# Six padded attention chunks, zero matmuls, split weight casts, and a last output tile in three column parts

## The chip, the cores and the metric

The kernel runs on one core of one Trainium2 chip. The metric is device time in microseconds (us), lower is better. Each kernel was run several times, always beside runs of the kernel before on the same chip. Runs have a state, fast or slow. The time is about 1.8 us longer than the "span" of the profile, which goes from the first instruction to the last.

Ratios are computed as the mean time of one kernel's fast runs over the mean of the other's of the same rounds, so they are not quite the ratio of the medians that are quoted. Intervals are 95%. A kernel counts as faster or slower when it differs by over 2%.

Engine names: PE is the TensorE matmul, PEld its weight load, DVE is VectorE, ACT is ScalarE, POOL is GpSimd, SP is SyncE, which here issues almost all DMAs.

## The reference

Attention with a decaying state, over 4 sequences of 768 tokens with 8 heads of 64 numbers, followed by a dense network of two layers:

```python
for b in range(nb):                       # blocks of 64 tokens
    intra = einsum('bhic,bhjc->bhij', qb, kb) * Dmask          # Dmask: lam ** (i - j), causal
    intra = einsum('bhij,bhjd->bhid', intra, vb)
    inter = einsum('bhid,bhde->bhie', qb * lam_pow, kv_state)
    out[:, :, sl] = intra + inter
    kv_state = lam_block * kv_state + einsum('bhsd,bhse->bhde', kb_dec, vb)
x = out.transpose(0, 2, 1, 3).reshape(3072, 512)
h = x @ w_in                              # 512 -> 2048
g = h * sigmoid(h)                        # silu
y = g @ w_out                             # 2048 -> 512, result 3072 x 512 float32
```

## The kernel before

The kernel works in bf16 on chunks of 128 tokens (24 of them) with float32 sums. Attention of a later group of chunks runs between the matmuls of the dense layers of an earlier group, so that PE always has something to do. The first group has four chunks; its attention is the start of the kernel.

Two heads share the 128 rows of PE. The first `N0 = 4` chunks use a *padded* layout: the values of a pair of heads lie in `vpad` beside zeros, and one ACT or DVE cast puts them there. All later chunks use *halves*: a cast to `vb`, then four DVE copies (`spread_v`) into a buffer that was cleared before. Halves need less PE time; padding needs no spreading. Buffers are used in turn, `c % 4`.

```python
NKV = 4                                   # vpad, ktbd, kvbd: four buffers each, cleared at the start
def spread_v(c):                          # only chunks that are not padded
    if c in vnew:
        vnew.discard(c)
        vb, vh = natb[c][2], vhalf[c % NKV]
        for j in range(2):
            for h in range(2):
                nc.vector.tensor_copy(vh[64*j:64*j+64, :, h, j, :], vb[64*h:64*h+64, :, j, :])

def pe_s(c, j, tag="att"):                # scores; a padded chunk takes all 128 columns
    qt, kt = tr[c]
    a = 0 if c < N0 else 64 * j
    # [...] four matmuls, one per pair of heads

def ffn1(g, m, ...):                      # one 128-row tile of h, then silu on ACT
def ffn2(g, mt, kos, tag="o"):            # out tile of 128 tokens x 512, 16 matmuls, DVE copy, store
    # [...]
    if kos[-1] == KO_OUT - 1:
        ob = opool.tile([128, DM], F32, tag="ob")
        nc.vector.tensor_copy(ob, o)
        stores.append([0, out[r0:r0 + BLK, :], ob])      # issued by SP a little later
def op_z(n, tag="kv"):                    # matmuls of zeros that nobody reads: they keep PE busy
    zero = kvbd[NKV - 1]
    for i in range(n):
        nc.tensor.matmul(wt, lhsT=zero[:, 0, :], rhs=..., start=True, stop=True)   # 512 columns

# the start is a list of words, executed in order: z zero matmuls, tq/tk transposes, s scores, m masks,
# d state, o output, x its cast, w:i cast of piece i of w_in, f:part,half first layer
ORDER = "z:8 pq:0,1,P pq:0,0,D tq:0,h [...] w:0,D d:2 [...] f:0,0 x:3,A w:1,D kv:3,A f:0,1 f:1,0 f:1,1 w:2,D w:3,D"

# the first switch from padding to halves, in program order
clear_halves()                            # POOL clears all four buffers again
[...]
st_s(5)
vcast(4), vcast(5)
spread_v(4), spread_v(5)                  # 8 copies on DVE
down0(3, 2)                               # dense layer 2, last quarter
st_d(4)
down0(3, 3)
st_o(4); st_d(5); next_prep()
down0(3, 0)
st_o(5); next_prep()
down0(3, 1)
stretch((ups(1), 0, 1), ([(vcast, 6), (spread_v, 6)], 0.0, 0.1), (pieces(2), 0.2, 1.15), ...)
[...]
for unit in downs(len(GROUPS) - 1, range(nch[-1])):      # the last tiles
    unit[0](*unit[1:])
tick(0)                                   # store of the last tile
```

## Time and profile before

| | before |
|---|---|
| time | 221.94 us median of 3 (221.92 to 222.25) |
| span of the profiled run | 219.35 us |
| PE busy | 205.9 us, 94% |
| first matmul; full clock in the trace's record from | 3.15; 11.87 us |
| first layer starts; its second group of matmuls | 20.64; 22.07 us |
| first matmul of group 1; scores of chunk 6 | 54.97; 59.56 us |
| end of PE; end of span | 215.61; 219.35 us |

The page of the kernel before, parts 1, 2 and 4 (busy time of an engine with its share and count; PE's busy tenths in 40 slices; the chain of waits by engine):

```profile
PE 205.9 (94%) x1595; PEld 127.4 (58%) x1595; DVE 122.5 (56%) x264; ACT 102.7 (47%) x213; POOL 62.1 (28%) x68
PE   4878999996799999999999999999999999999993
...
PE 83%; DVE 10%; ACT 3%; DMA 2%; issue 1%; POOL 1%; DVEq 0%
```

PE bounds the kernel. There are gaps only in three places, which the windows of the kernel before show (stretch in us, its length, then busy time of PE, PEld, DVE, ACT, POOL with instruction counts, clock, DMA share, GB/s):

```profile
0.00:22.00 22.00, 15.94 (x143) 10.22 (x143) 18.45 (x33) 13.75 (x26) 16.81 (x25) 1.00 1.04 234
...
43.00:66.00 23.00, 19.70 (x198) 14.12 (x196) 19.21 (x43) 12.53 (x27) 9.11 (x9) 1.00 1.20 232
66.00:100.00 34.00, 33.83 (x318) 24.52 (x316) 27.55 (x60) 17.59 (x43) 12.18 (x12) 1.00 1.18 202
100.00:208.00 108.00, 108.00 (x793) 64.44 (x791) 46.60 (x114) 49.29 (x101) 17.33 (x17) 1.00 0.59 117
208.00:219.00 11.00, 7.61 (x38) 3.43 (x35) 2.08 (x3) 0.38 (x1) 0.00 (x0) 1.00 0.18 72
```

PE lacks 6 us of work in the first 22 us, 3.3 us between 43 and 66, and the tail after 215.6 us has none. From 66 to 208 us it lacks 0.2 us in all.

The start, from the timeline of PE and DVE before (start, us, engine, line, operation, out<-in, count; in brackets the idle time before it and what ended it):

```profile
3.15 3.60 PE L489 MATMUL warm_ps<-kvbd 128*128 128x512 bf16 x8 [3.15 <-DVE kvbd L108]
...
21.10 0.92 DVE L159 CAST w_in_bf<-w_tmp 128x1024 bf16<-128x1024 f32 x1
...
22.07 1.16 PE L417 MATMUL h_ps<-xt,w_in_bf 128*128 128x256 bf16 x9 [0.39 <-DVE w_in_bf L159]
```

The second w_in piece landed at 20.20 us, but DVE reached its cast at 21.10. The middle, in the same views:

```profile
48.68 3.31 DVE L274 COPY vpad<-vb 64x256 bf16<-64x256 bf16 x8
...
50.84 0.55 PE L394 MATMUL op<-ss,vpad 128*128 128x128 bf16 x8 [0.61 <-DVE vpad L274]
...
53.54 0.40 PE L394 MATMUL op<-qt,kvbd 128*128 128x128 bf16 x4 [1.29 <-DVE kvbd L159]
...
54.97 2.11 PE L417 MATMUL h_ps<-xt,w_in_bf 128*128 128x256 bf16 x16
...
55.90 2.39 DVE L274 COPY vpad<-vb 64x256 bf16<-64x256 bf16 x4
...
59.56 0.51 PE L363 MATMUL sp<-qt,ktbd 128*128 128x128 bf16 x8 [1.16 <-DVE ktbd L159]
```

Spreading occupies DVE while PE waits, once for the copies themselves and twice for casts queued behind them. The tail, timeline before:

```profile
212.91 3.79 SPq L435 DMA_DIRECT2D out_dram<-ob  x2
215.64 0.69 DVE L447 COPY ob<-o_ps 128x512 f32<-128x512 f32 x1 [2.76 <-PE o_ps L443]
```

After the last matmul come a copy of 0.69 us and the second of these two stores, issued at 216.36 and landed 2.01 us later.

### The profile page before, as it was taken

What the parts mean: (1) busy time and instruction counts of PE and PEld (TensorE: products, weight loads), DVE (VectorE), ACT (ScalarE), POOL (GpSimd) and SP (SyncE); (2) the same over time, 40 slices, a digit from 0 to 9 for tenths busy, and PEclk for the clock granted to TensorE, in tenths of its full rate; (3) what the DMA queues carried; (4) which work ended last, traced back from release to release, by engine and by line L of the source; (5) the groups of instructions that cost most, each with busy time, mean ns of one, the idle gap of its engine ahead of it and who ended that gap; (6) DMA issues with size and microseconds to landing.
All of it is one profiled execution on the core that took longest, in us unless ns stands there. A gap on an engine that the chain in (4) does not pass through costs nothing.

```text
span 219.3 us, 4154 instructions
## 1 busy us (share of the span) xinstructions
PE 205.9 (94%) x1595; PEld 127.4 (58%) x1595; DVE 122.5 (56%) x264; ACT 102.7 (47%) x213; POOL 62.1 (28%) x68
## 2 busy tenths in 40 slices
PE   4878999996799999999999999999999999999993
PEld 1456644553695777775665566556655565566641
DVE  7699555089888768886686564436571341100021
ACT  4685564142673555655554454445445434433300
POOL 7579600716333332323333334203000000000000
PEclk9999999999999999999999999999999999999999
DMA  4999999999999999999999999949510011011112
GB/s 122 242 221 351 381 387 341 263 232 219 234 232 187 215 194 175 220 202 197 190 173 215 240 169 233 201 115 190 107 48 34 14 51 49 0 51 48 48 56 88
DMA packets 97652, 38.03 MB, mean 173 GB/s; under 512 B 86880, under 2 KB 90976, under 8 KB 97632
## 3 DMA queue, kind: packets, MB, share of 16 engines
q1 hardware_dynamic: 97488, 37.76, 81.1%
q8 instruction: 12, 0.20, 0.4%
q14 instruction: 8, 0.07, 0.1%
q10 hardware_dynamic: 144, 0.00, 0.0%
HBM read 27.27 MB, written 6.29 MB: 153 GB/s over the span
## 4 chain that ended last, share of the span: by engine, by line
PE 83%; DVE 10%; ACT 3%; DMA 2%; issue 1%; POOL 1%; DVEq 0%
PE o_ps L443 37%; PE h_ps L417 35%; PE op L394 5%; PE sp L363 4%; DVE ss L370 3%; DVE vpad L274 2%; DMA lam_sb<-in_lam_dram 2%; PE kv_ps L339 2%; ACT g L421 1%; DVE ktbd L159 1%; DVE ob L447 1%; DVE w_in_bf L159 1%; POOL qb L232 1%; DVE vpad L159 1%; ACT L127 1%
## 5 line engine op out<-in xcount | busy, mean ns | idle before, releaser
L421 ACT ACTIVATE g<-h_ps 128x256 bf16<-128x256 f32 (+2 forms) x144 | 65.1, 456 | 79.5 <-PE h_ps L417 78.1
L417 PE MATMUL h_ps<-xt,w_in_bf 128*128 128x256 bf16 (+2 forms) x592 | 99.9, 304 | 1.0 <-DVE w_in_bf L159 0.7
L443 PE MATMUL o_ps<-w_out_bf,g 128*128 128x512 bf16 x384 | 95.8, 379 | 0.2 <-DVE w_out_bf L159 0.2
L417 PEld LDWEIGHTS <-w_in_bf 128*128 128x128 bf16 x592 | 55.4, 98 | 32.6 <-issue 1.3
L443 PEld LDWEIGHTS <-g 128*128 128x128 bf16 x384 | 36.4, 98 | 32.2 <-issue 0.3
L447 DVE COPY ob<-o_ps 128x512 f32<-128x512 f32 x24 | 16.5, 691 | 47.1 <-PE o_ps L443 47.0
L243 POOL TENSOR_TENSOR qb<-qf,lam_fwd 128x512 bf16<-128x512 f32 x18 | 19.0, 1055 | 67.9 <-DMA qf<-in_q_dram 63.3
L370 DVE TENSOR_TENSOR ss<-sp,mask 128x512 bf16<-128x512 f32 (+1 forms) x48 | 25.7, 575 | 17.2 <-PE sp L363 16.5
L274 DVE COPY vpad<-vb 64x256 bf16<-64x256 bf16 x80 | 29.0, 362 | 1.8
L237 POOL TENSOR_TENSOR kb<-kf,lam_bwd 128x512 bf16<-128x512 f32 x23 | 24.3, 1060 | 6.0 <-DMA kf<-in_k_dram 4.1
L159 DVE CAST kvbd<-kv_ps 64x256 bf16<-64x256 f32 x32 | 13.5, 421 | 9.6 <-PE kv_ps L339 9.4
L402 ACT ACTIVATE xt<-op 128x512 bf16<-128x512 f32 x20 | 11.9, 597 | 11.0 <-PE op L394 10.3
L363 PEld LDWEIGHTS <-ktbd 128*128 128x128 bf16 x192 | 11.8, 100 | 6.2 <-DVE ktbd L159 2.9
L363 PE MATMUL sp<-qt,ktbd 128*128 128x128 bf16 (+1 forms) x192 | 13.7, 213 | 1.7 <-DVE ktbd L159 1.6
L394 PE MATMUL op<-ss,vpad 128*128 128x128 bf16 (+1 forms) x192 | 12.5, 208 | 0.6 <-DVE vpad L274 0.6
L157 ACT ACTIVATE vb<-vf 128x512 bf16<-128x512 f32 x20 | 12.5, 624 | 0.7 <-DMA vf<-in_v_dram 0.6
L159 DVE COPY ktbd<-kn 64x512 bf16<-64x512 bf16 x32 | 12.2, 382 | 0.8 <-DMA kn<-kb 0.5
L394 PEld LDWEIGHTS <-vpad 128*128 128x128 bf16 x192 | 10.7, 98 | 1.1 <-DVE vpad L274 0.8
L232 POOL TENSOR_TENSOR qb<-qf,lam_fwd 128x512 bf16<-128x512 f32 x4 | 4.6, 1166 | 16.6 <-DMA qf<-in_q_dram 15.0
L394 PE MATMUL op<-qt,kvbd 128*128 128x128 bf16 x80 | 7.7, 219 | 1.3 <-DVE kvbd L159 1.3
L159 DVE CAST w_in_bf<-w_tmp 128x1024 bf16<-128x1024 f32 x8 | 6.2, 781 | 3.8 <-DMA w_tmp<-in_moe_w_in_dram 3.8
L489 PE MATMUL warm_ps<-kvbd 128*128 128x512 bf16 x11 | 5.3, 632 | 3.2 <-DVE kvbd L108 3.2
(58 smaller groups left out, 85.4 us busy)
## 6 DMA issues: line engine op xcount, KB each, us to landing
kf<-in_k_dram SPq DMA_DIRECT2D x24, 256.0 KB, 4.8
vf<-in_v_dram SPq DMA_DIRECT2D x24, 256.0 KB, 5.1
out_dram<-ob SPq DMA_DIRECT2D x24, 256.0 KB, 3.1
qf<-in_q_dram SPq DMA_DIRECT2D x18, 256.0 KB, 3.7
w_tmp<-in_moe_w_in_dram SPq DMA_DIRECT2D x8, 512.0 KB, 8.6
w_tmp<-in_moe_w_out_dram SPq DMA_DIRECT2D x8, 512.0 KB, 10.1
qf<-in_q_dram SPq DMA_DIRECT2D x3, 512.0 KB, 5.9
qt<-qb SPq DMA_TRANSPOSE x16, 3.7
```

Source lines behind the costliest of these rows:

```text
L157: nc.scalar.activation(dst, src, AF.Copy)
L159: nc.vector.tensor_copy(dst, src)
L237: VG[e].tensor_tensor(kb, rawk.pop(c).rearrange("s (p j) d -> s p j d", j=2), decay(lam_bwd, c % NB), op=AL.mult)
L243: nc.gpsimd.tensor_tensor(qb, rawq.pop(c).rearrange("s (p j) d -> s p j d", j=2), decay(lam_fwd, c % NB), op=AL.mult)
L274: nc.vector.tensor_copy(vh[64 * j:64 * j + 64, :, h, j, :], vb[64 * h:64 * h + 64, :, j, :])
L363: nc.tensor.matmul(sp[:, p, :], lhsT=lhsT, rhs=qt[:, p, a:], start=True, stop=True)
L370: VG[e].tensor_tensor(ss, sp, m[:, None, :n].to_broadcast([128, 4, n]), op=AL.mult)
L394: nc.tensor.matmul(dst, lhsT=lhsT, rhs=rhs, start=(i == 0), stop=(i >= len(terms) - NP), skip_group_check=True)
L417: nc.tensor.matmul(hp[:, a:z], lhsT=w_in_bf[:, ko, m * 128:(m + 1) * 128], rhs=xt[g][:, ko, a:z], start=(ko == 0 and a == 0), stop=(ko == ...
L421: nc.scalar.activation(gg, hp[:, :n], AF.Silu)
L443: nc.tensor.matmul(o, lhsT=gt[g, ko][:, mt * BLK:(mt + 1) * BLK], rhs=w_out_bf[:, ko, :], start=(ko == 0), stop=(ko == KO_OUT - 1))
L447: nc.vector.tensor_copy(ob, o)
```

## The change

The intent has four parts.

1. *Padding to six chunks.* `NPAD = 6` in place of `N0 = 4`, so chunks 4 and 5 need no spreading. Their buffers 0 and 1 are then cleared for halves only after chunk 5 is done. The spread of chunk 6 moves later.
2. *Zero matmuls.* The zeroed weights come first, 15 zero matmuls instead of 8 at the start, and more in waits: 26 in all instead of 11, so that PE's clock rises early and stays up.
3. *Split casts.* The first two w_in pieces are cast half by DVE and half by ACT.
4. *Last tile in parts.* Columns 0–256, 256–384 and 384–512 each have their own bank, copy and store, so the last copy and store are small.

The core of the diff, with cuts marked:

```diff
+NPAD = 6
-z:8 pq:0,1,P pq:0,0,D tq:0,h [...] w:0,D d:2 kv:2,A o:2,att x:2,D
-d:3 o:3,att f:0,0 x:3,A w:1,D kv:3,A f:0,1 f:1,0 f:1,1 w:2,D w:3,D
+z:15 pq:0,1,P pq:0,0,D tq:0,h pk:0,D pk:1,P z:2 tk:0,o z:2 [...] z:1 [...] z:2 [...] z:1,o [...] z:2,o [...]
+o:2,att x:2,D w:0,DA z:1,o d:3 o:3,att f:0,0 x:3,A w:1,DA kv:3,A f:0,1 f:1,0 f:1,1 w:2,D w:3,D
+    nc.vector.memset(kvbd[NKV - 1], 0.0)          # the zero weights, now first
     def cast_w(which, i, e="D"):
-        move(e, w_piece(...), wtmp.pop((which, i)))
+        dst, t = w_piece(...), wtmp.pop((which, i))
+        n = dst.shape[1] // len(e)
+        for h, x in enumerate(e):
+            move(x, dst[:, n * h:n * h + n, :], t[:, n * h:n * h + n, :])
     [... c < N0 becomes c < NPAD at eight places; st_s uses mask if c < NPAD else mask2 ...]
-    clear_halves()
+    clear_halves(2, 3)
     [...]
     vcast(4), vcast(5)
-    spread_v(4), spread_v(5)
     [...]
     st_o(5)
     next_prep()
+    clear_halves(0, 1)
     down0(3, 1)
-    stretch((ups(1), 0, 1), ([(vcast, 6), (spread_v, 6)], 0.0, 0.1), (pieces(2), 0.2, 1.15),
+    stretch((ups(1), 0, 1), ([(vcast, 6)], 0.0, 0.1), ([(spread_v, 6)], 0.42, 0.42), (pieces(2), 0.2, 1.15),
+    def ffn2_last(g, mt):
+        for i, (a, z, tag) in enumerate([(0, 256, "o"), (256, 384, "h"), (384, 512, "h")]):
+            o = psum.tile([128, 512], F32, name="o_part", tag=tag, bufs=2)
+            [... 16 matmuls into o[:, :z - a] ...]
+            move("A" if i == 1 else "D", ob[:, :z - a], o[:, :z - a])
+            tick(0)
+            nc.sync.dma_start(out=out[r0:r0 + BLK, a:z], in_=ob[:, :z - a])
-    for unit in downs(len(GROUPS) - 1, range(nch[-1])):
+    for unit in downs(len(GROUPS) - 1, range(nch[-1] - 1)):
         unit[0](*unit[1:])
-    tick(0)
+    ffn2_last(len(GROUPS) - 1, nch[-1] - 1)
```

More of the change, by code (lines that the diff above doesn't have):

```diff
@@ L21 @@
 NQ2 = 6
+NPAD = 6
 ORDER = """
-z:8 pq:0,1,P pq:0,0,D tq:0,h pk:0,D pk:1,P tk:0,o z:1 kt:0,1,D qt:0,A kt:0,0,D qt:1,A s:0,1,o tk:1,h m:0,1,D pq:2,0,D
-s:0,0,att z:2 pq:2,1,P kt:1,0,A s:1,0,o tq:2,att kt:1,1,A pk:2,P m:0,0,D qt:2,A s:1,1,h vc:0,A tk:2,att m:1,0,D
-m:1,1,D d:0 qt:3,A pk:3,P kt:2,1,D s:2,1,h kt:2,0,D kv:0,A o:0,att s:2,0,h m:2,1,D tk:3,o m:2,0,D vc:1,A d:1 x:0,A
-kt:3,0,D kv:1,A s:3,0,att o:1,att kt:3,1,D s:3,1,h vc:2,D m:3,0,D vc:3,D x:1,A m:3,1,D w:0,D d:2 kv:2,A o:2,att x:2,D
-d:3 o:3,att f:0,0 x:3,A w:1,D kv:3,A f:0,1 f:1,0 f:1,1 w:2,D w:3,D
+z:15 pq:0,1,P pq:0,0,D tq:0,h pk:0,D pk:1,P z:2 tk:0,o z:2 kt:0,1,D qt:0,A kt:0,0,D qt:1,A s:0,1,o z:1 tk:1,h m:0,1,D
+pq:2,0,D s:0,0,att z:2 pq:2,1,P kt:1,0,A s:1,0,o tq:2,att kt:1,1,A pk:2,P m:0,0,D qt:2,A s:1,1,h vc:0,A tk:2,att
+m:1,0,D m:1,1,D d:0 qt:3,A pk:3,P kt:2,1,D s:2,1,h kt:2,0,D kv:0,A o:0,att s:2,0,h m:2,1,D z:1,o tk:3,o m:2,0,D vc:1,A
+z:2,o d:1 x:0,A kt:3,0,D kv:1,A s:3,0,att o:1,att kt:3,1,D s:3,1,h vc:2,D m:3,0,D vc:3,D x:1,A m:3,1,D d:2 kv:2,A
+o:2,att x:2,D w:0,DA z:1,o d:3 o:3,att f:0,0 x:3,A w:1,DA kv:3,A f:0,1 f:1,0 f:1,1 w:2,D w:3,D
 """
@@ L106 @@
         nc.vector.memset(vpad[i], 0.0)
-        if i == 1:
-            nc.vector.memset(kvbd[NKV - 1], 0.0)
         nc.vector.memset(ktbd[i], 0.0)
@@ L161, in cast_w @@
     def cast_w(which, i, e="D"):
-        move(e, w_piece(which, i, None, w_in_bf if which == "in" else w_out_bf), wtmp.pop((which, i)))
+        dst, t = w_piece(which, i, None, w_in_bf if which == "in" else w_out_bf), wtmp.pop((which, i))
+        n = dst.shape[1] // len(e)
+        for h, x in enumerate(e):
+            move(x, dst[:, n * h:n * h + n, :], t[:, n * h:n * h + n, :])
     mask2 = const.tile([128, BLK], F32)
@@ L170, with clear_halves @@
     khalf = [t.rearrange("d p j s -> d p (j s)").rearrange("d p (h j s) -> d p h j s", h=2, j=2) for t in ktbd]
-    def clear_halves():
-        for i in range(NKV):
+    def clear_halves(*bufs):
+        for i in bufs:
             nc.gpsimd.memset(ktbd[i], 0.0)
             nc.gpsimd.memset(vpad[i], 0.0)
-        for j in range(2):
-            nc.gpsimd.tensor_copy(mask2[64 * j:64 * j + 64, :], mask[0:64, :])
     NBUF = {"att": 3, "h": 2, "o": 2, "kv": 1}
@@ L190 @@
     xt = {}
-    N0 = GROUPS[0] // BLK
     def load_q(c):
@@ L238, in prep_k @@
                                 op=AL.mult)
-        natb[c] = (None, kb, vpad[c % NKV] if c < N0 else nat.tile([128, NP, 2, D], BF16, name="vb", tag="vb", bufs=2))
+        natb[c] = (None, kb, vpad[c % NKV] if c < NPAD else nat.tile([128, NP, 2, D], BF16, name="vb", tag="vb", bufs=2))
     def prep(c):
@@ L248, in vcast @@
     def vcast(c, e="A"):
-        if c in vraw and c >= N0:
+        if c in vraw and c >= NPAD:
             vb = natb[c][2]
@@ L284, in move_k @@
         rows = slice(64 * j, 64 * j + 64)
-        if c < N0:
+        if c < NPAD:
             move(e, ktbd[c % NKV][rows, :, j, :], t[rows, :, :])
@@ L304, in copy_qt @@
              tp[:, :, :, 64 * i:64 * i + 64].rearrange("d r p s -> d p s r"))
-        tr[c] = (qt, ktbd[c % NKV] if c < N0 else khalf[c % NKV])
+        tr[c] = (qt, ktbd[c % NKV] if c < NPAD else khalf[c % NKV])
     def pe_tk(c, tag):
@@ L338, in pe_d @@
         for p in range(NP):
-            nc.tensor.matmul(kv[:, p, :], lhsT=kb[:, p, :, :], rhs=vb[:, p, 0:4:3, :] if c < N0 else vb[:, p, :, :],
+            nc.tensor.matmul(kv[:, p, :], lhsT=kb[:, p, :, :], rhs=vb[:, p, 0:4:3, :] if c < NPAD else vb[:, p, :, :],
                              start=(blk == 0 and p == 0), stop=True, skip_group_check=True)
@@ L358, in pe_s @@
         qt, kt = tr[c]
-        a = 0 if c < N0 else 64 * j
+        a = 0 if c < NPAD else 64 * j
         sp = psum.tile([128, NP, BLK - a], F32, name="sp", tag=tag, bufs=NBUF[tag], padded_shape=[128, NP, BLK])
         for p in range(NP):
-            lhsT = kt[:, p, j, :] if c < N0 else kt[:, p, j, :, :]
+            lhsT = kt[:, p, j, :] if c < NPAD else kt[:, p, j, :, :]
             nc.tensor.matmul(sp[:, p, :], lhsT=lhsT, rhs=qt[:, p, a:], start=True, stop=True)
@@ L374, in st_s @@
         spread_k(c)
-        st[c] = [masked(pe_s(c, j), m=mask2) for j in range(2)]
+        st[c] = [masked(pe_s(c, j), m=mask if c < NPAD else mask2) for j in range(2)]
     def pe_o(c, tag="att"):
@@ L387, in pe_o @@
         for j in range(2):
-            if c < N0:
+            if c < NPAD:
                 terms += [(vb[:, p, 2 * j:2 * j + 2, :], res[j][:, p, :], op[:, p, :]) for p in range(NP)]
@@ L449, in ffn2 @@
             stores.append([0, out[r0:r0 + BLK, :], ob])
+    def ffn2_last(g, mt):
+        r0 = gstart[g] + mt * BLK
+        for i, (a, z, tag) in enumerate([(0, 256, "o"), (256, 384, "h"), (384, 512, "h")]):
+            o = psum.tile([128, 512], F32, name="o_part", tag=tag, bufs=2)
+            for ko in range(KO_OUT):
+                nc.tensor.matmul(o[:, :z - a], lhsT=gt[g, ko][:, mt * BLK:(mt + 1) * BLK], rhs=w_out_bf[:, ko, a:z],
+                                 start=(ko == 0), stop=(ko == KO_OUT - 1))
+            ob = opool.tile([128, DM], F32, name="ob", tag="ob")
+            move("A" if i == 1 else "D", ob[:, :z - a], o[:, :z - a])
+            tick(0)
+            nc.sync.dma_start(out=out[r0:r0 + BLK, a:z], in_=ob[:, :z - a])
     nch = [n // BLK for n in GROUPS]
@@ L514, in next_prep @@
                 load_c(loads.pop(0))
-    clear_halves()
+    clear_halves(2, 3)
+    for j in range(2):
+        nc.gpsimd.tensor_copy(mask2[64 * j:64 * j + 64, :], mask[0:64, :])
     for i in range(4, 8):
```

## The prediction

> **What bounds the kernel now.** TensorE is busy 94% of the 219.3 us span (page, engine table); the chain of waits puts 83% on PE. By stages (windows): from 66 to 208 us PE is busy 141.8 of 142 us, so nothing is to be had there. The change can win at three places: 0–22 us (PE busy 15.9 of 22, DVE 18.5), 43–66 us (PE 19.7 of 23), and the tail after 208 us.
>
> **Start.** Matmuls begin at 3.15 us at half pace (128 columns every 107 ns); the trace's first clock record, and a pace of 56 ns, begin at 11.87 us. The Trainium skill, "TensorE: Matmul & The Clock Gate", Part 1, says the gate opens after one busy free-running window of about 3.4 us; the trace agrees: PE is broken by idle pieces from 6.5 to 8.4 us, then nearly unbroken for 3.4 us. The zeroed weights now come first on DVE (ready near 1.3 us instead of 3.1) and 15 padding matmuls follow, so I expect full clock between 5 and 8.3 us. That shortens tk and sp on the chain by about 0.35 us; DVE paces the rest (busy 90–100% from 11 to 22). Later padding only fills waits. Split casts: the second w_in half is ready near 21.3 instead of 22.02 us (its DMA lands at 20.2), so ffn1's second group starts 0.65 us earlier. Later weight pieces land every 1.36 us, still in time.
>
> **43–66 us.** The spread copies of chunks 4 and 5 (8 DVE copies, 3.31 us at 48.7) vanish. They caused PE waits of 0.61 us (vpad) and 1.29 us (kvbd queued behind them); the spread of chunk 6 (2.39 us at 55.9), now behind the masks, caused 1.16 us (ktbd, 59.56). Against this: two masks grow from 415 to 689 ns, and the w_out cast queued behind them lets the last quarter of down-projection start only 0.3 us earlier. Walking both queues with these durations, ffn1 of group 1 starts at 52.7 instead of 54.97 us and sp of chunk 6 at 56.5 instead of 59.56. Kept by 66 us: 2.8 us. Clearing buffers 0 and 1 on POOL (four memsets of 0.95–1.5 us) now precedes chunk 8's preparation, which slips from 58 to about 61 us; its transposes were issued at 61.3 anyway: a few tenths at most.
>
> **Tail.** Before: last matmul ends 215.6, copy 0.69 us, store issued 216.36, landed 218.37. After: about 0.1 us more on PE; last copy 128 columns (estimate 0.29 us, from the 691 ns of 512 columns and 259 ns of 96); last store 64 KB instead of 256. "DMA: Bandwidth & Descriptors" puts most of a small transfer into a fixed part; the trace has 2.0 us for 256 KB, so I count 0.3 us off. Tail gain 0.6 us.
>
> **Sum.** 2.8 + 0.6 = 3.4 us: 218.5 us, 217.2 to 219.9. Chances: faster 0.15, within 2% 0.84, slower 0.01.
>
> **What would show it.** Clock record before 8.5 us; ffn1's second group near 21.4; no vpad copies at 48–52; PE idle in 43–66 falling from 3.3 to about 1 us; 66–208 unchanged but 2.8 us earlier; last copy 0.3 us, last landing 1.7 us after issue.
>
> **What would make it wrong.** DMA arrivals (loads of chunks 6–9 land 3.6–5 us apart, DMA share over 0.9 until 145 us) stalling the pulled-in PE at 60–80 us; POOL memsets slowing DVE spread copies (0.94 to 2.4 us under POOL work); the clock window falling late, so that padding delays tk; or DVE's queue giving more at the start than I count.

## The result, and the profile after

The kernel after takes 219.59 us (median of 4 runs, 219.19 to 220.11) against 222.09 us (4 runs, 221.92 to 222.26) of the kernel before: ratio 0.9891, interval 0.9864 to 0.9918. A second measurement, a0_again below, gave 0.9932, 0.9907 to 0.9957. By these two measurements the change saves 1.5 to 2.5 us, under 2%.

The profiled run, at 220.11 us the slowest of the four (spans of the other three: 217.5 to 217.8 us), is set against a profiled run of the kernel before that took 221.05 us, less than any of its timed runs. So these two profiles, whose spans are 1.03 us apart, understate the change. The profiled run after has this page (parts 1, 2 and 4 again):

```profile
PE 207.6 (95%) x1642; PEld 129.7 (59%) x1642; DVE 109.8 (50%) x257; ACT 103.9 (48%) x216; POOL 59.7 (27%) x68
PE   7778899999899999999989999999999999999994
...
PE 47%; DMA 30%; SPq 14%; POOL 5%; issue 1%; DVE 1%; POOLq 0%
```

Slice 10 is now full and slice 11 nearly so, and slice 21, full before, now has an 8. The chain of waits no longer lies on PE alone: 44% of it are DMAs and their issue. The windows after, of the stretches that changed:

```profile
0.00:22.00 22.00, 17.07 (x158) 10.36 (x158) 16.99 (x33) 13.85 (x26) 14.00 (x23) 1.00 1.03 233
...
43.00:66.00 23.00, 21.70 (x221) 15.76 (x219) 16.72 (x37) 12.51 (x27) 13.21 (x14) 1.00 1.17 233
...
100.00:208.00 108.00, 107.08 (x781) 63.60 (x779) 43.85 (x113) 48.33 (x99) 18.71 (x18) 1.00 0.63 123
```

Busy PE time does not tell progress here, as zero matmuls count as busy. A ledger does: the same instruction in several profiles, as its shift against the kernel before (a minus is earlier). The expected column is worked out from the prediction; "again" is a0_again, "best" is g1_dveclear, an experiment below.

| instruction | before, us | expected | after | again | best |
|---|---|---|---|---|---|
| second group of the first layer | 22.07 | −0.65 | +0.41 | +0.13 | +0.10 |
| first layer of group 1 begins | 54.97 | −2.27 | −1.42 | −1.66 | −1.66 |
| scores of chunk 6 | 59.56 | −3.06 | −1.82 | −2.06 | −2.06 |
| second layer of group 1 begins | 65.85 | −2.8 | −1.32 | −0.93 | −2.06 |
| last scores | 179.91 | −2.8 | −0.14 | −0.72 | −1.66 |
| end of PE | 215.61 | −2.7 | −0.06 | −0.64 | −1.58 |
| end of span | 219.35 | −3.4 | −1.03 | −1.62 | −2.57 |

The gain of the middle is there, but smaller, the start gained nothing, and in the profiled run most of the middle's gain went away before the last scores.

*Start.* The trace's record of full clock begins at 4.55 us instead of 11.87. The timeline of PE and DVE after:

```profile
1.26 5.02 PE L504 MATMUL warm_ps<-kvbd 128*128 128x512 bf16 x15 [1.26 <-DVE kvbd L104]
...
21.88 0.54 DVE L160 CAST w_in_bf<-w_tmp 128x512 bf16<-128x512 f32 x1 [1.76 <-DMA w_tmp<-in_moe_w_in_dram]
...
22.48 0.72 PE L419 MATMUL h_ps<-xt,w_in_bf 128*128 128x256 bf16 x5 [1.25 <-DVE w_in_bf L160]
```

DVE is now free at 20.1 us and waits 1.76 us for the second w_in piece, which landed at 21.85 us; before, it landed at 20.20.

*Middle.* No spreading at 48 us; the timeline of PE, DVE and POOL after:

```profile
53.55 1.67 PE L419 MATMUL h_ps<-xt,w_in_bf 128*128 128x256 bf16 x12
...
57.74 0.51 PE L365 MATMUL sp<-qt,ktbd 128*128 128x128 bf16 x8 [0.41 <-DVE ktbd L160]
...
58.32 1.04 POOL L245 TENSOR_TENSOR qb<-qf,lam_fwd 128x512 bf16<-128x512 f32 x1
...
59.17 1.76 DVE L276 COPY vpad<-vb 64x256 bf16<-64x256 bf16 x4
...
63.08 0.51 PE L365 MATMUL sp<-qt,ktbd 128*128 128x128 bf16 x8 [0.32 <-DVE ktbd L160]
```

The wait at 59.56 us before fell from 1.16 to 0.41 us, and a new one of 0.32 us came at 63.08 us. The preparation of chunk 8, at 55.6 us before, now stands at 58.32 behind the four memsets.

*Late.* A wait that the kernel before has not, in the timelines of DVE and PE:

```profile
112.15 0.59 DVE L160 COPY ktbd<-kn 64x512 bf16<-64x512 bf16 x2 [2.90 <-DMA kn<-kb]
...
112.80 0.51 PE L365 MATMUL sp<-qt,ktbd 128*128 128x128 bf16 x8 [0.92 <-DVE ktbd L160]
```

The same scores before, timeline of PE:

```profile
112.95 0.50 PE L363 MATMUL sp<-qt,ktbd 128*128 128x128 bf16 x8
```

The transposed keys of chunk 15 landed at 112.13 us, 5.11 us after their issue; before, at 108.62, 2.81 us after it. What the record shows of the difference is told at g3_best below.

*Tail.* The timeline after:

```profile
214.25 1.99 SPq L464 DMA_DIRECT2D out_dram<-ob  x3
214.69 0.28 ACT L158 ACTIVATE ob<-o_part 128x128 f32<-128x128 f32 x1 [5.65 <-PE o_part L459]
215.59 0.29 DVE L160 COPY ob<-o_part 128x128 f32<-128x128 f32 x1 [1.36 <-PE o_part L459]
```

From the end of PE to the end of the span it takes 2.77 us instead of 3.74. The last store of 64 KB landed 1.56 us after its issue.

### The profile page after: what moved, and what is told of

The parts are those of the page before. It is cut to its first block, busy times and chain, and to the rows that moved or that the text cites. A ratio compares the mean times of both kernels' runs of the same rounds, so it can differ in the third digit from the quotient of the medians.

```text
span 218.3 us, 4252 instructions
## 1 busy us (share of the span) xinstructions
PE 207.6 (95%) x1642; PEld 129.7 (59%) x1642; DVE 109.8 (50%) x257; ACT 103.9 (48%) x216; POOL 59.7 (27%) x68
## 4 chain that ended last, share of the span: by engine, by line
PE 47%; DMA 30%; SPq 14%; POOL 5%; issue 1%; DVE 1%; POOLq 0%
PE o_ps L445 22%; PE h_ps L419 19%; DMA qf<-in_q_dram 16%; SPq L209 8%; DMA w_tmp<-in_moe_w_in_dram 5%; DMA w_tmp<-in_moe_w_out_dram 5%; POOL qb L245 4%; SPq L263 3%; DMA kn<-kb 2%; PE op L396 2%; SPq L153 2%; DMA kf<-in_k_dram 2%; PE o_part L459 2%; PE sp L365 1%; POOL kb L239 1%
## 5 line engine op out<-in xcount | busy, mean ns | idle before, releaser
L445 PE MATMUL o_ps<-w_out_bf,g 128*128 128x512 bf16 x368 | 92.3, 379 | 0.3 <-DVE w_out_bf L160 0.3
L445 PEld LDWEIGHTS <-g 128*128 128x128 bf16 x368 | 34.9, 98 | 30.5 <-issue 0.5
L449 DVE COPY ob<-o_ps 128x512 f32<-128x512 f32 x23 | 15.9, 692 | 43.5 <-PE o_ps L445 43.4
L276 DVE COPY vpad<-vb 64x256 bf16<-64x256 bf16 x72 | 18.3, 254 | 1.6
L160 DVE COPY ktbd<-kn 64x512 bf16<-64x512 bf16 x32 | 10.8, 339 | 10.7 <-DMA kn<-kb 10.4
L365 PEld LDWEIGHTS <-ktbd 128*128 128x128 bf16 x192 | 11.2, 98 | 6.9 <-DVE ktbd L160 3.9
L158 ACT ACTIVATE vb<-vf 128x512 bf16<-128x512 f32 x18 | 11.2, 622 | 0.0
L234 POOL TENSOR_TENSOR qb<-qf,lam_fwd 128x512 bf16<-128x512 f32 x4 | 4.6, 1166 | 20.1 <-DMA qf<-in_q_dram 18.5
L504 PE MATMUL warm_ps<-kvbd 128*128 128x512 bf16 x26 | 8.5, 453 | 1.3 <-DVE kvbd L104 1.3
L160 DVE CAST w_in_bf<-w_tmp 128x1024 bf16<-128x1024 f32 (+1 forms) x8 | 5.2, 644 | 6.1 <-DMA w_tmp<-in_moe_w_in_dram 6.1
L341 PEld LDWEIGHTS <-kb 128*128 128x128 bf16 x80 | 6.1, 98 | 3.3 <-issue 0.9
```

Of the source, the lines that this page charges most:

```text
L160: nc.vector.tensor_copy(dst, src)
L276: nc.vector.tensor_copy(vh[64 * j:64 * j + 64, :, h, j, :], vb[64 * h:64 * h + 64, :, j, :])
L365: nc.tensor.matmul(sp[:, p, :], lhsT=lhsT, rhs=qt[:, p, a:], start=True, stop=True)
L445: nc.tensor.matmul(o, lhsT=gt[g, ko][:, mt * BLK:(mt + 1) * BLK], rhs=w_out_bf[:, ko, :], start=(ko == 0), stop=(ko == KO_OUT - 1))
```

## The experiments

Twelve runs, in four jobs, each job on one chip beside 11 runs of the kernel before. The medians of the kernel before were 221.37, 221.2, 222.04 and 221.46 us in the four jobs.

### The parts alone

Theory: the change's parts add up, and each keeps its own gain. Rival: one part takes away what another gives, or one part does all.

**a0_again** is the kernel after, unchanged. Its expectation already names theory F, that fetches of instructions delay loads, and rival L, that the new waits were luck of one run.

> The changed kernel once more, unaltered. The first profile of it had two TensorE waits that the kernel before lacked: 1.4 us at 21 us for the second piece of w_in (landed at 21.85 instead of 20.20 us) and 1.1 us at 112 us for kn (landed at 112.1 instead of 108.6 us). Theory F: both come from 16 KiB instruction fetches (at 19.69 and 108.13 us) that fall just before these loads land, and the place of a fetch is set by the instruction count, so at least the first wait recurs in this profile (second piece landing after 21.3 us). Rival L: they are luck of that one run, the second piece lands near 20.2 us here and the profiled span is 1 to 2 us shorter. Time over before: 0.989 either way.

Measured: 219.71 us (219.34 to 220.78), ratio 0.9932. The profile has no wait at 112 us, since these keys landed at 110.84. But the four spread copies of chunk 6 took 2.39 us, and the wait of chunk 7's scores became 0.93 us. So the wait at 112 us varies from run to run. The lost start does not: the w_in piece landed at 21.64, as theory F expected. Timelines of DVE and PE, a0_again:

```profile
58.93 2.39 DVE L276 COPY vpad<-vb 64x256 bf16<-64x256 bf16 x4
...
63.47 0.51 PE L365 MATMUL sp<-qt,ktbd 128*128 128x128 bf16 x8 [0.93 <-DVE ktbd L160]
...
112.24 0.50 PE L365 MATMUL sp<-qt,ktbd 128*128 128x128 bf16 x8
```

**b_tail** is the kernel before with the last part alone.

```diff
-    for unit in downs(len(GROUPS) - 1, range(nch[-1])):
+    for unit in downs(len(GROUPS) - 1, range(nch[-1] - 1)):
         unit[0](*unit[1:])
-    tick(0)
+    ffn2_last(len(GROUPS) - 1, nch[-1] - 1)
```

> Kernel before plus only the last tile in three parts. Both theories: 0.6 to 0.75 us faster (ratio 0.997); the last store lands about 1.6 us after its issue instead of 2.0, the last copy takes 0.29 us instead of 0.69. Nothing earlier than 208 us changes.

Measured: 220.92 us (220.08 to 221.84), ratio 0.9982, 0.9956 to 1.0007. From the end of PE to the end of the span 3.18 us, 0.56 less than before, where the whole change gave 0.97 less. The three last stores landed 3.23, 2.67 and 1.98 us after issue; 1.6 was expected for the last. A packet of 16 KiB of the kind "instruction" on queue q8 started at 215.54 us, between them; in the kernel after it starts at 213.90. Such packets are what theory F is about.

**b_start** is the kernel before with the new order, the early zero weights and the split casts.

```diff
-z:8 pq:0,1,P [...] w:0,D [...] w:1,D
+z:15 pq:0,1,P [...] w:0,DA [...] w:1,DA
+    nc.vector.memset(kvbd[NKV - 1], 0.0)
```

> Kernel before plus only the start: zero weights first, the padding, the split casts. As predicted blind: second group of ffn1 at 21.4 us instead of 22.07, 0.65 us faster at most (ratio 0.997 to 0.999). Theory F: the 15 extra padding matmuls (30 instructions) pull the instruction fetch ahead of the landing of the second w_in piece, so that piece lands after 21.3 us, the second group starts at 22.3 to 22.6 us, and this part alone gains nothing or loses up to 0.5 us (ratio 1.000 to 1.003).

Measured: 220.94 us (220.79 to 221.41), ratio 0.9986, 0.9966 to 1.0006. Full clock from 5.97 us, but the second w_in piece at 21.08 (theory F expected it after 21.3) and the second group at 22.41 us, 0.34 us later than before. The late piece is not the whole of this delay. Timeline of DVE, b_start:

```profile
20.24 2.12 DVE L158 CAST w_in_bf<-w_tmp 128x512 bf16<-128x512 f32 x2
```

The second of these two casts is DVE's half of the second piece. It started on the landing, at 21.11 us, but lasted 1.25 us beside a memset of POOL (20.86 to 22.08), where it lasts 0.54 us in the kernel after; ACT's half was done at 21.73. So POOL's clearing of the buffers holds up the split cast as it holds up the spread copies below.

**b_npad** is the kernel before with the padding of chunks 4 and 5, the moved clear and the moved spread.

```diff
+NPAD = 6            # c < N0 becomes c < NPAD
-    clear_halves()
+    clear_halves(2, 3)
-    spread_v(4), spread_v(5)
+    clear_halves(0, 1)     # after the second next_prep
-    ([(vcast, 6), (spread_v, 6)], 0.0, 0.1)
+    ([(vcast, 6)], 0.0, 0.1), ([(spread_v, 6)], 0.42, 0.42)
```

> Kernel before plus only the padded chunks 4 and 5, the later clearing of buffers 0 and 1 and the later spread of chunk 6. Predicted: 2.0 to 2.3 us faster at 66 us and at the end (ratio 0.990). If the supply of transposes (loop of loads and transposes through one queue) binds near 112 us, about 1 us of that comes back as a wait for kn there and the ratio is 0.994 to 0.995.

Measured: 220.43 us (219.67 to 221.55), ratio 0.9965, 0.9935 to 0.9996. Group 1 began at 52.97 us, 2.00 us earlier. By the last scores 0.46 us of that were left: the spread copies of chunk 6 took 3.21 us, and PE waited 0.67 us for them (until 61.86 us) and 0.93 us for the keys of chunk 7 behind them (until 63.95 us). The wait for late keys near 112 us, which the expectation allowed for, did not come.

The product of the three ratios, 0.9982 x 0.9986 x 0.9965 = 0.9933, is that of the whole in this job, 0.9932. Within their intervals the parts add up, but each interval is 0.4 to 0.6% wide, so this is a weak test. The start gives nearly nothing and the middle keeps a quarter of what it gained by the last scores, so most of the loss lies within the parts and not between them.

### Why the second w_in piece is late

A piece is one DMA that is counted in as 16 arrivals. The trace gives each arrival's time. Second piece, in us (the last three of 16, sorted), and the first 16 KiB packet of the kind "instruction" on queue q8:

```text
                    packet starts   last three of 16 arrivals    first piece with a lone late arrival
before                 20.23         20.02  20.15  20.20          third (21.68, then 22.60)
after                  19.69         20.30  20.67  21.85          second
a0_again               18.33         20.06  20.12  21.64          second
b_start                17.62         20.25  20.29  21.08          second
```

Fifteen arrivals come nearly as before, one comes 0.8 to 1.5 us after the fifteenth, and from there on one arrival is late in every piece that follows. The pages of both kernels list 12 and 13 packets on q8, 0.20 and 0.21 MB, all of the kind "instruction". The Trainium skill, "Runtime: NRT & Kernel Launch", section "Instruction fetch mechanics", says that an engine's instructions are refilled in blocks of 16 KiB, 256 instructions, by the sequencer's own DMA queue. The traces agree: PE and PEld together have 3190 instructions before and 3284 after, 266 and 253 per packet. The 15 more zero matmuls are 30 more instructions, and the packet starts 0.5 to 2.6 us earlier in the three profiles with them. The packet itself took 0.93, 1.00 and 1.04 us in these three traces, about as long as the late arrival is late.

The table has four of the 14 kept profiles; the others draw the same line. The second piece landed at 21.08 to 21.85 us in eight of the nine profiles whose packet started by 19.7 us (the ninth is f1_tiny, below), and at 20.12 to 20.84 in the five whose packet started later.

Theory F: the fetch of PE's instructions delays one of the 16 parts of the piece being loaded, and the padding moved it onto the second piece. Rival: earlier traffic or the other order of casts delays the piece.

**f1_tiny** is the kernel before with 16 zero matmuls of 8 columns, which cost almost no PE time but move the fetch.

```diff
-[...] m:2,1,D tk:3,o m:2,0,D vc:1,A d:1 [...]
+[...] m:2,1,D y:8,o tk:3,o m:2,0,D vc:1,A y:8,o d:1 [...]
```

> Kernel before plus 16 zero matmuls of 8 columns (32 TensorE instructions, about 0.03 us each) in two waits of TensorE near 13.3 and 15.5 us; nothing else. Theory F (instruction fetch): TensorE reaches the next 16 KiB block earlier, the fetch is asked for before 19.5 us instead of 20.2 to 20.5, the second w_in piece lands at 21.1 to 21.9 us instead of 20.2 to 20.9, and the second group of ffn1 starts at 22.3 to 22.8 us instead of 21.9 to 22.07: 0.3 to 0.7 us later for work that fits into waits. Rival D (the changed order of DVE and ACT work delays the piece): nothing moves, piece at 20.2 to 20.9 us, second group at 22.0 us.

Measured: 221.09 us (220.56 to 222.68), ratio 1.0003, 0.9977 to 1.0028. The packet started at 19.44 us, 0.8 us earlier, but the second piece came at 20.27 us, and the first lone late arrival was still in the third piece. The expectation of theory F failed.

**f2_fewz** is the kernel after with 12 zero matmuls at the start and none later.

```diff
-z:15 [...] z:2 [...] z:2 [...] z:1 [...] z:2 [...] z:1,o [...] z:2,o [...] z:1,o [...]
+z:12 [...]
```

> Changed kernel with 12 padding matmuls at the start and none later: as many TensorE instructions ahead of ffn1 as in the kernel before (136 matmuls instead of 150). Theory F: fetch back at 20 us or later, second w_in piece at 20.2 to 20.9 us, second group of ffn1 at 21.3 to 21.7 us instead of 22.2 to 22.5, TensorE ends 0.6 to 1.0 us before the changed kernel's. Rival D: second piece still after 21.3 us. If the later padding was needed for the clock, the clock record would start near 9 us or later, or a half-clock record would appear, and this kernel is 0.3 us or more slower.

Measured: 220.13 us (219.34 to 222.04), ratio 0.9963, 0.9927 to 0.9999. The packet started at 20.72 us, and the second piece landed at 20.13, the third at 21.61; the lone late arrival first shows in the fourth. Here theory F held. f4_both, below, has the same edit and agrees: packet at 21.39, second piece at 20.12, first lone late arrival in the fourth. But the second group came at 22.17 us all the same (22.07 in f4_both), as the two halves of the second cast were ready only at 22.08 and 22.11. ACT's half stood behind the cast of an attention output that came 0.8 us later than in the kernel after. DVE's half, begun at 20.87, lasted 1.25 us beside a memset of POOL. So a piece that lands in time does not bring the predicted start by itself. PE was late there after a stretch of half clock. Windows of f2_fewz around it (the third number from the right is the granted clock):

```profile
11.00:14.47 3.47, 1.97 (x27) 1.36 (x25) 3.41 (x6) 2.11 (x5) 2.18 (x3) 1.00 1.37 217
14.47:17.88 3.41, 3.15 (x32) 2.89 (x30) 2.65 (x6) 2.53 (x6) 1.51 (x2) 0.50 1.23 266
17.88:21.00 3.12, 2.83 (x47) 2.53 (x46) 2.75 (x7) 1.90 (x5) 1.29 (x2) 1.00 1.07 374
```

After 3.47 us with PE busy for 1.97 us the clock was half for 3.41 us. All six runs of f2_fewz have a mean granted clock of 0.982 to 0.992, while all ten of the kernel after have 0.999 or 1.000. So without the later zero matmuls (and three of those at the start) the clock falls in this start, and with them the fetch comes early. For the second group it came to nearly the same: 22.17 us without, 22.48 and 22.20 with them.

**g2_tiny38** repeats f1_tiny with more: 38 tiny matmuls, earlier.

```diff
-[...] tk:2,att m:1,0,D [...] vc:1,A d:1 [...]
+[...] tk:2,att y:24,o m:1,0,D [...] vc:1,A y:14,o d:1 [...]
```

> Kernel before with 38 zero matmuls of 8 columns (76 TensorE instructions) in the waits of TensorE at 13.1 and 15.6 us; nothing else. Theory F: the fetch of the next instruction block starts before 19.0 us (20.2 to 20.5 us in the kernel before, 19.4 with 16 of them), and one of the 16 arrivals of the second w_in piece comes 0.8 to 1.5 us after the other fifteen, so the piece lands at 21.1 to 21.9 us and the second group of ffn1 starts at 22.3 to 22.7 us instead of 22.05. Rival D (the late arrival in the changed kernel has to do with its other edits): all 16 arrivals of the second piece lie within 1.0 us, and the straggler shows first in the third piece, as in the kernel before.

Measured: 221.77 us (220.93 to 222.4), ratio 0.9999, 0.9964 to 1.0034. The packet started at 15.90 us. Late arrivals came already in the first piece (14 by 18.69, then 19.34 and 19.78 us) and in the second (14 by 20.07, then 20.72 and 21.16). The landing was as expected, in a kernel whose casts are those of before, though two arrivals were late and not one. The later second group was not: it came at 22.09, since in that order DVE reaches this cast only at about 21.1 us anyway. The old order had about 0.9 us of slack against a late piece; the new one has none.

Three of four profiles made to test it (f2_fewz, f4_both, g2_tiny38) moved the late arrival with the fetch; f1_tiny did not. Which piece a packet meets is not settled by its start alone: 19.44 us met the third piece and 19.69 us the second. Some late arrivals of about half a microsecond also come before any packet: in the first piece of b_tail (0.46 us after the fifteenth, packet at 20.31) and of b_npad (0.70 us, packet at 20.49). So the fetch is not the only thing that makes an arrival late.

### The spread copies and GpSimd

The prediction counted 2.39 us for the spread of chunk 6 and allowed for more under POOL's memsets. Theory P: those memsets push the preparation of chunk 8 onto the copies, and if the clear comes after this preparation, the copies are free.

**f3_lateclear** does that; **f4_both** adds the edit of f2_fewz.

```diff
             if c >= NPET:
                 dma_t(c)
+            if c == 8:
+                clear_halves(0, 1)
[...]
     next_prep()
-    clear_halves(0, 1)
     down0(3, 1)
```

> Changed kernel with the clearing of buffers 0 and 1 moved behind the preparation of chunk 8 on POOL. Theory P (POOL tensor_tensor work slows the DVE spread copies of chunk 6): the preparation of chunk 8 runs at 56.8 to 59 us instead of 58.3 to 60.8, the four spread copies of chunk 6 take 0.95 to 1.5 us instead of 1.8 to 2.4, the wait of sp for ktbd at 62.3 us (0.5 to 1.1 us) falls under 0.3 us, and TensorE is 0.3 to 0.8 us earlier at 66 us. Rival: the wait is DVE's own queue (masks, spread, kvbd in a row); moving POOL work changes it by under 0.2 us.

> Both edits together. If both theories hold they add: TensorE 1.0 to 1.8 us earlier at 66 us than in the changed kernel, time 218.2 to 219.0 us, that is 0.985 of the kernel before, unless the supply of transposes through one queue gives it back as a wait for kn near 105 to 115 us.

Measured: f3_lateclear 223.21 us (222.86 to 225.43), ratio 1.0113, 1.0076 to 1.0151; f4_both 222.77 us (221.07 to 224.10, its five fast runs), ratio 1.007, 1.0033 to 1.0106. The opposite of what was expected. Timelines of POOL, DVE and PE of f3_lateclear:

```profile
58.26 0.95 POOL L179 MEMSET ktbd<- 128x1024 bf16 x1
...
60.93 0.95 POOL L180 MEMSET vpad<- 128x1024 bf16 x1
61.85 1.04 POOL L245 TENSOR_TENSOR qb<-qf,lam_fwd 128x512 bf16<-128x512 f32 x1
62.85 1.04 POOL L239 TENSOR_TENSOR kb<-kf,lam_bwd 128x512 bf16<-128x512 f32 x1
...
58.94 5.29 DVE L276 COPY vpad<-vb 64x256 bf16<-64x256 bf16 x4
...
64.03 0.55 PE L396 MATMUL op<-ss,vpad 128*128 128x128 bf16 x8 [2.72 <-DVE vpad L276]
```

Four copies that take 0.94 us alone took 5.29 us. Taken one by one, the copies lasted 3.02, 1.00, 0.98 and 0.22 us, and ended at 61.96, 62.97, 63.97 and 64.22: the first at the end of the row of memsets (61.88), the next two each at the end of a multiplication (62.89 and 63.89), the last at once. In a0_again the first two ended at 59.83 and 60.83, where POOL's multiplications ended at 59.75 and 60.75. The Trainium skill, "SBUF — State Buffer", section "SBUF: two separate sides", says that VectorE, in some of its modes, and GpSimd share a pair of ports as an exclusive lock, which whoever starts first holds for its whole instruction. The copies agree with it, with about 0.1 us from the end of POOL's instruction to the end of the copy. A row of memsets let no copy in between; two multiplications in a row let one in.

The wait of 2.72 us then cost more than itself: the clock was half from 65.28 to 72.10 us, and PE ended 4.80 us later than before. Theory P fell: not which POOL work comes first matters, but how long POOL's whole row is.

**g1_dveclear** therefore takes the memsets off POOL. DVE does them, where it is idle.

```diff
-    def clear_halves(*bufs):
+    def clear_halves(*bufs, e=nc.gpsimd):
         for i in bufs:
-            nc.gpsimd.memset(ktbd[i], 0.0)
-            nc.gpsimd.memset(vpad[i], 0.0)
+            e.memset(ktbd[i], 0.0)
+            e.memset(vpad[i], 0.0)
[...]
     next_prep()
-    clear_halves(0, 1)
+    clear_halves(0, e=nc.vector)
     down0(3, 1)
+    clear_halves(1, e=nc.vector)
```

> Changed kernel with the four clearing memsets of buffers 0 and 1 on DVE (idle from 54.4 to 56.5 us there) instead of POOL. Theory P2 (any POOL work, memsets above all, holds up DVE's spread copies; f3_lateclear made that worse, 5.3 us for four copies): POOL prepares chunk 8 by about 59 us, the four spread copies of chunk 6 take 0.95 to 1.3 us, the wait of sp of chunk 7 near 62.3 us falls from 0.5 to 1.1 us to under 0.3 us, TensorE is 0.3 to 0.8 us earlier at 66 us. Rival Q (the wait is only the length of DVE's own queue): the wait stays over 0.45 us although the copies are short. Ratio over before 0.986 to 0.991.

Measured: 218.71 us (218.16 to 219.58), ratio 0.9864, 0.9831 to 0.9896. This is the lowest time. Its interval overlaps the first one of the kernel after (0.9864 to 0.9918), so that the times alone do not settle that it is faster; the ledger shows where it is. Timeline of DVE of g1_dveclear:

```profile
54.89 0.48 DVE L180 MEMSET vpad<- 128x512 uint32 x1
58.93 1.11 DVE L276 COPY vpad<-vb 64x256 bf16<-64x256 bf16 x4
```

A memset takes DVE 0.48 us, POOL 0.95. The preparation of chunk 8 is done by 59.23 us, so it delays the copies by 0.17 us only. The wait for the scores of chunk 7 is gone, and the ledger keeps all of the 2.06 us from the scores of chunk 6 to the second layer of group 1, where a0_again fell from 2.06 to 0.93.

### The order of the first layer, and the keys at 110 us

**g3_best** is g1_dveclear with the two halves of the first layer that need only the first w_in piece before the others.

```diff
-f:0,0 x:3,A w:1,DA kv:3,A f:0,1 f:1,0 f:1,1
+f:0,0 x:3,A w:1,DA kv:3,A f:1,0 f:0,1 f:1,1
```

> g1_dveclear plus another order of ffn1's first four half-groups: both that need only the first w_in piece first, then both that need the second. If the late second piece is what costs the start its gain, TensorE works 0.9 us longer before it waits, ffn1 starts its third quarter of work at the landing of the second piece as before but with 0.87 us of work already done, and the first down-projection starts at 34.8 to 35.2 us instead of 35.65 to 35.9; some of it is lost again to the load of q of chunk 4 (landing at 40.2 us), so 0.3 to 0.8 us is left at 66 us. Time 0.3 to 0.8 us under g1_dveclear, ratio over before 0.983 to 0.988.

Measured: 219.31 us (217.77 to 219.76), ratio 0.9879, 0.9844 to 0.9914. The second layer began at 35.27 instead of 35.66 us, so the order works, though 34.8 to 35.2 was expected. Here the first piece came late (19.63 us) and DVE's half of its cast lasted 1.27 us beside POOL's memsets; h1_actstore, below, has the same order and began at 34.77. But PE then waited at 111 us. Timeline of PE, g3_best:

```profile
111.52 0.51 PE L365 MATMUL sp<-qt,ktbd 128*128 128x128 bf16 x8 [0.63 <-DVE ktbd L160]
```

The keys of chunk 15 landed at 110.85 us, in g1_dveclear at 110.61 with a wait of 0.23 us. The time is not better than that of g1_dveclear: the intervals overlap for the most part. A theory for the keys: they come at the pace of SP's queue, in which loads, DMA transposes and stores stand in one order, and a PE that is 2 us ahead of the kernel before meets this pace.

The traces hold a rival, theory F, which the expectation of a0_again had named for these keys too and which no edit followed up. The transpose of these keys took 4.19 to 5.19 us in the six profiles in which a 16 KiB packet on q8 started within 2 us after its issue, a time shorter than any of these transposes (after, a0_again, b_start, f2_fewz, g1_dveclear, g3_best), and 2.59 to 3.78 us in the other eight. Of all 224 such transposes in the 14 profiles, the 54 with a packet in flight have a median of 4.3 us, the other 170 one of 2.8. In the kernel after the packet started at 108.13 us, in the kernel before at 110.68, after the landing. No edit tested this alone, so it is a pattern across all profiles and not a proven cause.

**h1_actstore** tests that: the stores go to ACT's queue.

```diff
-            nc.sync.dma_start(out=dst, in_=ob)
+            (nc.scalar if late else nc.sync).dma_start(out=dst, in_=ob)
```

Rival: ACT is held up by the stores' own waits.

> g3_best with the stores of the output tiles before the last issued by ScalarE instead of SyncE, so that the loads and DMA transposes no longer share SyncE's order with the stores. If the order of SyncE's DMAs is what makes the transposed keys of chunk 15 late, they land at least 1 us earlier than in g3_best (at or before 109.6 us instead of 110.85), TensorE's wait at 110.6 us (0.79 us in g3_best) falls below 0.2 us, and the time is 0.4 to 0.8 us under g3_best (ratio 0.982 to 0.987). Rival: ScalarE is held up by the stores' own waits, silus come later, TensorE gets new waits on ScalarE's tiles, and the time is that of g3_best or worse.

Measured: 226.42 us (225.22 to 227.21), ratio 1.0203, 1.0161 to 1.0246: slower, but whether by over 2% is unclear. The keys of chunk 15 landed at 106.74 us, 4.1 us earlier than in g3_best, and their wait is gone. That part is as expected, but it does not prove the pace: PE was itself late by then, the transpose was issued only 1.69 us earlier, and the other 2.41 us are a shorter transpose (2.77 instead of 5.19 us) with no packet in it. The rival's cost decided. Timeline of ACT and PE of h1_actstore:

```profile
85.86 0.34 ACTq L437 DMA_DIRECT2D out_dram<-ob  x1
86.25 0.66 ACT L423 ACTIVATE g<-h_ps 128x256 bf16<-128x256 f32 x2 [3.02 <-DMA qf<-in_q_dram]
86.68 0.60 PE L419 MATMUL h_ps<-xt,w_in_bf 128*128 128x256 bf16 x4 [1.61 <-ACT g L423]
```

ACT stood for 3.02 us until a load of q landed at 85.78, then issued the store, then the silu that PE waited for. There were five such waits of PE for silu, of 1.06 to 1.61 us each and 6.7 us in all, ending between 72 and 120 us. That is far more than the 0.63 us that the late keys had cost.

### What the zero matmuls are worth

Each run lists its mean granted clock. Of 44 runs of the kernel before in the four jobs, 9 have 0.985 and a mean of 222.5 us; the other 35, at 0.989 and above, have a mean of 221.3. All ten runs of the kernel after have 0.999 or 1.000. So part of what the padding gives may not show in any single profile: on average 1.2 us x 9/44 = 0.24 us, if it is the padding that keeps this variant away. That agrees with b_start, whose six runs have 0.996 to 1.000.

The start of full clock is partly luck. The five profiles with the old start (before, b_tail, b_npad, f1_tiny and g2_tiny38, whose first 13 us are the same) have it at 11.87, 11.86, 12.34, 7.39 and 6.71 us; the nine with the new one at 4.2 to 7.3. The Trainium skill, "TensorE: Matmul & The Clock Gate", Part 1, says that the clock is granted by windows of about 3.4 us which run free of the kernel. The records agree: the half clocks lasted 3.41 us in f2_fewz and 6.8 us, two windows, in f3_lateclear, and the same start opened the clock at 6.7 us in one run and at 12.3 in another.

## Why the prediction was right, and where its terms were off

The prediction said 218.5 us (217.2 to 219.9), within 2%. The measured 219.59 us lies inside the range, near its upper end. The saving was predicted at 3.4 us and measured at 2.5, and at 1.5, less than half, in the second measurement. By its steps:

- **"Full clock between 5 and 8.3 us"**: right, with 4.55 and 5.53 us.
- **"ffn1's second group starts 0.65 us earlier"**: wrong; it started 0.41 and 0.13 us later. The failed premise is "its DMA lands at 20.2". That number came from the profile before, and the change itself moved it to 21.85 and 21.64. The runs show one of 16 arrivals late, and three of four test profiles moved it together with the fetch of PE's instructions. So "later padding only fills waits" failed with it. The DVE time was freed as predicted: DVE waited 1.76 us for the piece. But a second premise is doubtful too, that the half is then cast at its usual speed: in f2_fewz and f4_both, whose piece came by 20.13 us, DVE's half lasted 1.25 us beside POOL's memset.
- **"ffn1 of group 1 starts at 52.7 instead of 54.97 us"**: right in mechanism; 53.55 and 53.31. The shortfall is 0.85 and 0.61 us, and the start alone is short by 1.06 and 0.78. In b_npad, which has the start of before, the middle alone brought 2.00 us (0.17 of them were there at the second group already), where the prediction's own 2.27, less its 0.65 for the start, is 1.62: this step was even a little under-sized.
- **"sp of chunk 6 at 56.5 instead of 59.56"**: 57.74 and 57.50. The gain from group 1 to these scores was predicted at 0.79 us and measured at 0.40.
- **"Kept by 66 us: 2.8 us"**: over-sized; 1.32 and 0.93. Besides the start, it is the clear on POOL, of which the prediction said "a few tenths at most". It pushed the preparation of chunk 8 onto the spread of chunk 6, which took 1.76 and 2.39 us, against 0.94 alone. From the scores of chunk 6 to 66 us the prediction gave up 0.26 us (3.06 less 2.8); the runs gave up 0.50 and 1.13, and with the clear on DVE nothing.
- **"66–208 unchanged"**: only in part. From 66 us to the last scores one profile lost 1.18 us, most of it to late keys at 112 us, the other 0.21. The prediction named DMA arrivals as a risk, but at 60 to 80 us.
- **"Tail gain 0.6 us"**: the path from PE's end to the span's end got 0.97 us shorter, less about 0.1 us more PE. Last copy 0.29 us as estimated, last landing 1.56 us instead of 1.7. The term was under-sized by 0.3 us. In b_tail, where a packet of the fetch starts within the tail, the path got only 0.56 us shorter.

So the sign and the parts were right, and the mechanism of the middle; the start's gain did not come. That the total still fell inside is in part luck: the range is 2.7 us wide, and the tail and the middle's first step, both under-sized, made up for some of the start and of the clear. What stays open is why the fetch meets one piece and not its neighbour, and an experiment that moves the fetch off the keys of chunk 15 alone; in the traces their landing, at 108.62 or at 112.13 us, goes with it.

## What to carry to other kernels

When a DMA landing is the next bound behind the one you remove, treat its time as part of the change and not as given: here, added instructions with no data came with a later landing. Keep long rows of GpSimd work away from the moments when VectorE's copies and casts are on the critical path; moving four memsets from GpSimd to VectorE, where it was idle, took away a loss of 0.50 to 1.13 us here, more than any reordering gained. In h1_actstore a store that waited its turn on ScalarE held up the silu behind it, so ask what else stands in a queue before giving it the stores.

## What the Trainium skill lacked or had wrong

- "Runtime: NRT & Kernel Launch", "Instruction fetch mechanics": the cost of a fetch is called mostly hidden, and for the engine itself no run here contradicts it. It lacks what a fetch goes with for the data under way: one of 16 arrivals of a 512 KB load came 0.8 to 1.5 us after the others (21.85 against 20.67 us for the fifteenth), a key transpose took 4.3 us in the median against 2.8, and the store of 128 KB in the tail landed 2.83 to 3.23 us after issue in the three profiles with a packet in it, against 1.81 to 2.39 in the other six.
- "SBUF — State Buffer", "SBUF: two separate sides": the lock is as the copies show it, but that a row of GpSimd memsets is not interrupted between its instructions is missing: one copy lasted 3.02 us across three memset ends (f3_lateclear), while between two multiplications one copy got in each time.
- "DMA: Bandwidth & Descriptors", "Anatomy of one DMA — SWDGE (gpsimd) path": its fit of 2.0 us plus bytes over 436 GB/s, made for another way of issuing DMAs, gives 2.6 us for 256 KB and 2.15 for 64 KB. The stores at the end took 2.01 and 1.56 us. The difference of 0.45 us fits the bytes; the fixed part is about 1.4 us here (2.01 − 0.60 = 1.41 and 1.56 − 0.15 = 1.41, estimates from these two landings and the page's rate).
- "TensorE: Matmul & The Clock Gate", "Why this matters for your kernels": it asks for no idle gaps over about 3 us. That did not suffice: in f2_fewz the clock was halved at 14.47 us although the longest idle stretch of PE in the 4.7 us before was 0.87 us; PE was busy for 1.97 of the last 3.47 us. Which busy share keeps the clock is not stated there, and no run here measures it.
